# An RWKV-5 block followed by a mixture-of-depths layer on one core: chosen rows turned a unit later, turns one unit ahead, head and tail in another order

## The chip, the cores and the metric

The kernel runs on one core of one Trainium2 chip. The metric is device microseconds of one execution. TensorE is called PE here (its weight loads PEld), VectorE DVE, ScalarE ACT, GpSimd POOL and SyncE SP, as the profile calls them.

## The reference

```python
# r, k, v: (4, 8, 768, 48); w, u: (8, 48)
for t in range(S):
    cur = np.einsum('bhd,bhe->bhde', u[None] * kt, vt)
    y[:, :, t] = np.einsum('bhd,bhde->bhe', rt, state + cur)
    state = w[None, :, :, None] * state + np.einsum('bhd,bhe->bhde', kt, vt)
# x: y as (4, 768, 384); w_gate (384), w1 (384, 1024), w2 (1024, 384), capacity 128
scores = np.einsum('bsd,d->bs', x, w_gate)
out = x.copy()
for b in range(B):
    top_idx = np.argpartition(-scores[b], capacity)[:capacity]
    xe = x[b, top_idx]
    ye = np.maximum(xe @ w1, 0.0) @ w2
    g = 1.0 / (1.0 + np.exp(-scores[b, top_idx]))
    out[b, top_idx] = x[b, top_idx] + g[:, None] * ye
```

So a recurrence over 768 steps for 4 batches of 8 heads gives x; then, in each batch, the 128 rows with the highest scores go through a two-layer network and are written back.

## The kernel before

**Units.** The 4 x 768 rows are cut into 24 units of 128 rows, six to a batch; a unit holds all 8 heads in two chunks of 64 rows. In a unit the recurrence is written as matrix products: r is scaled by powers of w (`rh`), k by inverse powers (`kh` by the way of `kw`, which is k times `wk`), `scores` forms the chunks' r-by-k products in the PSUM tile `rp`, `masked` copies their lower triangle over a diagonal matrix `at` (which `diagonal` fills with the u-bonus `du` of the rows), `values_part` multiplies `at` with v into the PSUM tile `y`, `states_part` adds r times the state before the chunk, `state_sums` and `states` make the next state (`z`, `g`), and `decays` scales it by `wc` with four ACT instructions. `leave_y` copies `y` to `x` with three ACT copies and stores it; SP issues that store. `mark` is a one-element ACT copy of `y` that stands between `states_part` and `values_part`: the values products wait for it.

**Order.** The schedule is by hand (`manual_schedule`): each engine does its instructions in the order in which the code writes them, and waits only for data and buffers. The main loop runs over i = 0 to 24. Pass i (called unit i below) does `states_part`, `mark`, `values_part`, `leave_y` and the gate score for unit i-1, and scores, sums, states and mask for unit i; then it transposes on PE (`turn`, into `pk` and `pr`) and scales the k and r of a unit ahead (`turned_k` on ACT, `turned_r` on DVE); POOL does the bonus products `rk` and `rku` of unit i+2, `diagonal` and `scaled` (`kw`). Loads of r, k and v are issued by SP four units ahead.

**The second layer.** `score_row`, `compare_own` and `compare_others` compare the scores of a batch's blocks (`gt`); three passes after a batch's last unit, `rank` sums them on PE and DVE gives each row its rank (`qq`) and six one-hot blocks (`oh`); a pass later `pick` turns them to row numbers (`idx`) and `fetch` reads the 128 chosen rows (`xr`) from the output in HBM with an indirect DMA that POOL issues. `chosen` transposes `xr` on PE into `m`, ACT copies it to `xt`, and a queue of 16 pieces (8 `hidden`, 6 matmuls of the trace each, and 8 `expert`, 2 each) is taken out 3, 3, 2, 3, 3, 2 to a pass, behind the turns. `leave` adds the result to the rows and `store_rows` writes them back, also by POOL. Batch 3's second layer stands behind the loop (the tail).

**Places.** The dictionary `fill` and the list `counts` set the pass of each step of the second layer; `PARTS` the passes in which SP issues the eight weight loads; `pieces(m)` takes m pieces from the queue.

Of the kernel before, what the change touches and what calls it, by code (L numbers as in the profile page):

```python
# [17 lines left out]
def kernel(  # L18
# [29 lines left out]
    NIN, NV, NKW = 6, 8, 5  # L48
# [24 lines left out]
    wrow = const.tile([NP, 2, PAD], F32)  # L73
    ub = const.tile([128, H, D], F32)
# [13 lines left out]
    def load(n, which="krv"):  # L88
# [196 lines left out]
    SR, GT, RS, QQ, XR, XT, IDX, GA, HT, OH = {}, {}, {}, {}, {}, {}, {}, {}, {}, {}  # L285
    out_rows = out.rearrange("b s d -> (b s) d")

    def score_row(n):
        b, c = divmod(n, NC)
        if c == 0:  # L290
# [3 lines left out]
            nc.vector.tensor_copy(RS[b][:, 1, :], off)  # L294
# [16 lines left out]
    def rank(b):  # L311
        p = PM[:, 128 : 128 + NC]
        for c in range(NC):
            for cc in range(c, NC):
                nc.tensor.matmul(out=p[:, c : c + 1], lhsT=GT[b][:, cc, c, :], rhs=ones,
                                                   start=(cc == c), stop=(cc == NC - 1))
        rs = work.tile([128, NC], F32, name="rsum")
        nc.vector.tensor_add(rs, RS[b][:, 0, :], RS[b][:, 1, :])
        nc.vector.tensor_add(rs[:, 1:], rs[:, 1:], off[:, 1:])  # L319
        QQ[b] = work.tile([128, NC], F32, name="qq")  # L320
        nc.vector.tensor_add(QQ[b], p, rs)
# [89 lines left out]
    def store_rows():  # L411
        while LEFT:
# [52 lines left out]
    turn(PR, rpads[0])  # L465
    nc.vector.tensor_copy(tr[:, :, C + 1 : C + 2], PM[:, :NP][:, :, None])
# [138 lines left out]
```

## Time and profile before

| | us |
|---|---|
| median of 3 runs | 178.82 (177.78 to 180.06) |
| the profiled execution | 178.97 |
| its span, first to last instruction | 177.2 |
| PE busy | 142.8 (81%) |
| DVE busy | 115.3 (65%) |
| POOL busy | 108.6 (61%) |
| ACT busy | 71.7 (40%) |

The span is what the profile shows; 1.77 us of the execution lie around it. A busy share is a mean over stages with different limits, so the reading goes by stretches. In the page's groups and in the timeline, a line gives start or count, duration, engine, code line, what is written and what is read, and in brackets the idle time before it and what ended it; "issue" is time in which the engine waited for nothing that the profile shows.

### The profile page before, as it was taken

The page shows a single profiled execution, that of the slowest core. Times are in us where ns is not written, and L with a number is a line of the kernel's source. Part 1 is how long each engine was busy: PE and PEld are TensorE (multiplying, and loading weights), DVE is VectorE, ACT ScalarE, POOL GpSimd, SP SyncE. Part 2 cuts the span into 40 slices and gives each one's busy share as a digit, 9 for nine tenths or more (in the row PEclk, how much of TensorE's full clock was granted, in tenths as well). Part 3 has the DMA queues.
Part 4 walks back from the last instruction along what each step waited for, and adds up shares of the span by engine and source line. Part 5 has one row for each costly group of instructions (what it writes and reads, how often), then busy time and mean ns, then how long its engine had stood idle before and what let it go on. Part 6 is the DMA issues. An engine that isn't in the chain of part 4 may idle for free.

```text
span 177.2 us, 8283 instructions
## 1 busy us (share of the span) xinstructions
PE 142.8 (81%) x3605; PEld 121.4 (69%) x3605; DVE 115.3 (65%) x332; ACT 71.7 (40%) x243; POOL 108.6 (61%) x132
## 2 busy tenths in 40 slices
PE   1659977676977938999999599999997698939880
PEld 1448866566776828999777399997785596619740
DVE  6968568879699942679899634798997256520010
ACT  3114455452566542436466242465552443011100
POOL 5499999988599595289985970989936000040002
PEclk9999999998798796999999858999999999996998
DMA  6899998869899898777979770476113111020001
GB/s 109 175 206 190 182 216 179 176 138 244 178 249 238 178 265 209 166 171 207 238 168 195 196 169 13 113 156 141 48 48 93 50 48 45 0 93 0 0 0 44
DMA packets 81871, 24.51 MB, mean 138 GB/s; under 512 B 75564, under 2 KB 81452, under 8 KB 81836
## 3 DMA queue, kind: packets, MB, share of 16 engines
q1 hardware_dynamic: 81024, 22.03, 55.1%
q0 software_dynamic: 512, 1.57, 2.6%
q10 hardware_dynamic: 300, 0.39, 1.6%
q8 instruction: 28, 0.46, 1.1%
q14 instruction: 7, 0.06, 0.1%
HBM read 18.48 MB, written 5.51 MB: 135 GB/s over the span
## 4 chain that ended last, share of the span: by engine, by line
PE 37%; issue 25%; DVE 17%; DMA 11%; ACT 6%; POOL 1%; POOLq 1%; DVEq 0%
PE y L219 9%; DMA xr<-out_dram,idx 8%; PE e L393 7%; PE pk L191 5%; PE pr L191 4%; PE rp L205 4%; PE e L400 3%; PE rp L246 2%; ACT z L261 2%; DVE rh L195 2%; DVE gt L308 2%; DMA rpad<-in_r_dram 2%; DMA wrow<-in_w_dram 2%; DVE rsum L319 2%; DVE at L210 1%
## 5 line engine op out<-in xcount | busy, mean ns | idle before, releaser
L186 POOL TENSOR_TENSOR at<-dia,du 128x512 f32<-128x512 f32 x24 | 25.0, 1043 | 23.8 <-DVE du L182 13.2
L178 POOL TENSOR_TENSOR rku<-rk,ub 128x384 f32<-128x384 f32 x24 | 24.8, 1033 | 1.9
L176 POOL TENSOR_TENSOR rk<-rpad,kin 128x384 f32<-128x384 f32 x23 | 25.9, 1125 | 0.1
L195 DVE TENSOR_TENSOR rh<-pr,tr 128x512 f32<-128x512 f32 x24 | 16.4, 685 | 14.3 <-PE pr L191 14.0
L393 PE MATMUL e<-xt,w 128*128 128x128 f32 x162 | 23.5, 306 | 2.6 <-ACT xt L370 2.6
L393 PEld LDWEIGHTS e<-xt,w 128*128 128x128 f32 x162 | 22.4, 222 | 3.2 <-ACT xt L370 3.0
L219 PE MATMUL y<-vin,at 64*64 64x48 f32 x768 | 18.6, 227 | 6.5 <-issue 5.1
L400 PE MATMUL e<-w,ht 128*128 128x384 f32 x64 | 22.7, 490 | 0.4 <-ACT ht L396 0.4
L172 POOL TENSOR_TENSOR kw<-kin,wk 128x384 f32<-128x384 f32 x22 | 22.3, 1014 | 0.0
L205 PE MATMUL rp<-rh,kh 48*64 48x64 f32 x768 | 19.5, 232 | 3.2 <-issue 2.4
L270 ACT COPY x<-y 128x192 f32<-128x192 f32 x24 | 7.6, 318 | 35.5 <-PE y L219 34.3
L219 PEld LDWEIGHTS y<-vin,at 64*64 64x64 f32 x768 | 15.8, 142 | 7.8 <-issue 5.8
L261 ACT ACTIVATE z<-g,wc 128x48 f32<-128x48 f32 x80 | 20.2, 323 | 2.0 <-DVE g L255 1.6
L205 PEld LDWEIGHTS rp<-rh,kh 48*64 48x64 f32 x768 | 16.1, 145 | 4.6 <-issue 3.2
L191 PE MATMUL pk<-ident,kw 128*128 128x128 f32 x92 | 17.5, 321 | 1.8 <-DVE kw L172 1.8
L282 DVE SCALAR_TENSOR_TENSOR scr<-x,wg 128x384 f32<-128x384 f32 x24 | 17.2, 718 | 1.7 <-ACT x L272 1.6
L191 PE MATMUL pr<-ident,rpad 128*128 128x128 f32 x96 | 17.2, 309 | 0.9 <-DMA rpad<-in_r_dram 0.9
L210 DVE COPY_PREDICATED at<-mask,rp 128x512 f32<-128x512 uint32 x24 | 17.5, 730 | 0.0
L219 PE MATMUL y<-z,rh 48*64 48x48 f32 x704 | 16.9, 225 | 0.0
L301 DVE SCALAR_TENSOR_TENSOR gt<-m,sc,tri 128x128 bf16<-128x128 f32 x24 | 8.3, 347 | 13.2 <-ACT srow L297 12.2
L219 PEld LDWEIGHTS y<-z,rh 48*64 48x64 f32 x704 | 13.9, 137 | 4.4 <-issue 2.2
L358 POOL DMA_INDIRECT xr<-out_dram,idx x4 | 4.2, 1049 | 19.1 <-DVE idx L340 18.8
(88 smaller groups left out, 235.2 us busy)
## 6 DMA issues: line engine op xcount, KB each, us to landing
rpad<-in_r_dram SPq DMA_DIRECT2D x24, 192.0 KB, 3.6
vin<-in_v_dram SPq DMA_DIRECT2D x24, 192.0 KB, 4.8
out_dram<-x SPq DMA_DIRECT2D x24, 192.0 KB, 3.5
kin<-in_k_dram SPq DMA_DIRECT2D x23, 192.0 KB, 3.7
w<-in_moe_w_dram SPq DMA_DIRECT2D x8, 384.0 KB, 4.6
kpad<-in_k_dram SPq DMA_DIRECT2D x1, 192.0 KB, 2.8
ub<-in_u_dram ACTq DMA_DIRECT2D x1, 192.0 KB, 4.7
wg<-in_moe_w_gate_dram ACTq DMA_DIRECT2D x1, 192.0 KB
```

What stands on the lines that cost most here:

```text
L172: engine.tensor_mul(kws[n % NKW][:, :, :D], KIN[n], wk)
L176: nc.gpsimd.tensor_mul(rk, rpads[n % NIN][:, :, :D], KIN[n])
L178: nc.gpsimd.tensor_mul(RKU[n], rk, ub)
L186: nc.gpsimd.tensor_mul(AT[n], dia[:, None, :].to_broadcast([128, H, C]), DU[n].rearrange("t i p -> t (i p)")[:, :, None].to_broadcast([128 ...
L191: nc.tensor.transpose(dst[:, hp, :], src[:, 2 * hp : 2 * hp + 2, :], ident)
L195: nc.vector.tensor_mul(RH[n], PR, tr[:, :, :T])
L205: nc.tensor.matmul(out=RP[half(c), i, hp * C : (hp + 1) * C], lhsT=KH[n][head(i), hp, half(c)], rhs=RH[n][head(i), hp, half(c)], start=Tru ...
L210: nc.vector.copy_predicated(at, causal, RP[:, :, : NP * C].rearrange("s i (p t) -> s i p t", p=NP))
L219: nc.tensor.matmul(out=y_out(hp, i, c), lhsT=lhsT, rhs=rhs, start=(n, i, c) not in begun, stop=True, skip_group_check=True)
L261: nc.scalar.activation(Z0[n + 1][:, hp, :], G[n][:, hp, :], AF.Copy, scale=wc[:, hp : hp + 1])
L393: nc.tensor.matmul(out=pe[:, (f - f0) * 128 : (f - f0 + 1) * 128], lhsT=w1[:, d, f * 128 : (f + 1) * 128], rhs=XT[b, z][:, d, :], start=(d ...
L400: nc.tensor.matmul(out=PE[:, :Dm], lhsT=HT[b, z][:, f, :], rhs=w2[:, f, :], start=(f == 0), stop=(f == FB - 1))
```

## The change

It touches four things.

- **Second layer.** `chosen`, `enqueue` and `gates` of batches 0 to 2 move from pass e+5 to e+6 (e is the batch's last unit), and the six passes with pieces with them; `fetch` stays in pass e+4, but behind `diagonal` and ahead of `scaled` on POOL; `store_rows` writes only what an earlier pass left. "small" steps (ranks, pick, chosen) run ahead of the mask.
- **Turns.** k and r are turned one unit ahead instead of two, ahead of `decays`; `kw`, `kh`, `rh` and `vin` lose a buffer each. Sums stand before scores. In passes up to 9, four of a unit's eight diagonal blocks are made by ACT with a scaled copy each (`at` of 64 columns), the rest by POOL.
- **Head.** `u` and the gate vector come as one row each and are spread over the partitions by a product with a row of ones (`spread`); PE does 8, 3 and 3 transposes that nobody reads (`idle`); `kt` is made in halves and turned ahead of the first scores; no unit is turned in pass 0.
- **Tail.** The ranks of batch 3 are summed for blocks 0 to 4 first and for block 5 later; more hidden pieces, and six of the eight expert pieces, stand elsewhere. Weights come two passes later at first (7 to 14 instead of 5, 7 to 13).

```diff
-    NIN, NV, NKW = 6, 8, 5
+    NIN, NV, NKW = 6, 7, 4
...
-    nc.scalar.dma_start(
-        out=ub, in_=bass.AP(tensor=u.tensor, offset=u.offset, ap=[[0, 128], [D, H], [1, D]])
-    )
+    nc.scalar.dma_start(out=vecs[:, 0, :], in_=u.rearrange("h d -> (h d)")[None, :])
+    nc.scalar.dma_start(out=vecs[:, 1, :], in_=moe_w_gate[None, :])
...
+    def idle(m):
+        for _ in range(m):
+            nc.tensor.transpose(YP[:, 0, :128], ident, ident)
+
+
+    def spread(dst, j):
+        nc.tensor.matmul(out=PE[:, :Dm], lhsT=line, rhs=vecs[:, j, :], start=True, stop=True)
+        nc.scalar.copy(dst, PE[:, :Dm])
...
+    def diagonal(n, first=0):
         AT[n] = work.tile([128, H, C], F32, name="at", bufs=4)
...
+        for h in range(first):
+            nc.scalar.activation(AT[n][:, h, :], dia, AF.Copy, scale=du[:, h : h + 1])
+        if first < H:
+            nc.gpsimd.tensor_mul(AT[n][:, first:, :], dia[:, None, :].to_broadcast([128, H - first, C]),
+                                 du[:, first:, None].to_broadcast([128, H - first, C]))
...
-    def store_rows():
-        while LEFT:
+    def store_rows(m):
+        for _ in range(m):
...
-            at(e + 5, "small", chosen, b, z)
-            at(e + 5, "small", enqueue, b, z)
-            at(e + 5, "gate", gates, b, z)
+            at(e + 6, "small", chosen, b, z)
+            at(e + 6, "small", enqueue, b, z)
+            at(e + 6, "gate", gates, b, z)
         for j in range(6):
-            counts[e + 5 + j] = STEP[j % 3] * NST
...
-    PARTS = (5, 7, 8, 9, 10, 11, 12, 13)
+    PARTS = (7, 8, 9, 10, 11, 12, 13, 14)
...
+    idle(8)
     nc.tensor.transpose(PM[:, :NP], wrow.rearrange("p i d -> p (i d)"), ident[:NP, :NP])
     turn(PK, kpad)
+    nc.vector.tensor_copy(tr[:, :, C + 1 : C + 2], PM[:, :NP][:, :, None])
+    spread(ub.rearrange("t h d -> t (h d)"), 0)
+    idle(3)
     turn(PR, rpads[0])
+    idle(3)
...
     for i in range(NU + 1):
+        left = len(LEFT)
...
+        if 0 < i and i + 1 < NU:
+            turn(PK, kws[(i + 1) % NKW])
+            turned_k(i + 1)
+            turn(PR, rpads[(i + 1) % NIN])
+            turned_r(i + 1)
         if i < NU:
             decays(i)
-
-        run(i, "small")
-        if i + 2 < NU:
-            turn(PK, kws[(i + 2) % NKW])
-            turned_k(i + 2)
-            turn(PR, rpads[(i + 2) % NIN])
-            turned_r(i + 2)
...
-        if i + 1 < NU:
-            diagonal(i + 1)
-        if i + 3 < NU:
-            scaled(i + 3, nc.gpsimd)
+        if 0 < i and i + 1 < NU:
+            diagonal(i + 1, 4 if i < 10 else 0)
         run(i, "pool")
-        store_rows()
+        store_rows(left)
+        if 0 < i and i + 2 < NU:
+            scaled(i + 2, nc.gpsimd)
...
     b = B - 1
+    last = NC - 1
+    rank(b, PK[:, 0, :], range(last))
+    compare_others(NU - 1)
+    rank_base(b)
+    nc.vector.tensor_add(RB[b][:, :last], RB[b][:, :last], PK[:, 0, :last])
     pieces(2)
     score_row(NU - 1)
-    compare_others(NU - 1)
     compare_own(NU - 1)
-    pieces(2)
-    rank(b)
+    rank_more(b)
+    pieces(1)
+    rank(b, PM[:, 128 : 128 + NC], range(last, NC))
+    rank_sum(b, PM[:, 128 : 128 + NC])
+    pieces(1)
     for z in range(NST):
         one_hot(b, z)
-        pieces(2)
         pick(b, z)
         fetch(b, z)
     pieces(len(queue))
```

Three places show how the rows stand on an engine. First PE in pass 10, the one after batch 0's rows are fetched, before the change (`m` from `xr` is `chosen`, `e` from `xt` the first three hidden pieces):

```order
L205 MATMUL rp<-rh,kh 64x64 x16
L246 MATMUL rp<-vin,kw_87 48x48 x16
L219 MATMUL y<-vin,at 64x48 x16
L367 MATMUL m<-ident,xr 128x128 x3
L191 MATMUL pk<-ident,kw_89 128x128 x4
L191 MATMUL pr<-ident,rpad_81 128x128 x4
L393 MATMUL e<-xt,w_75 128x128 x9
L295 MATMUL m<-ident,sc_142 128x128
```

With the change pass 10 has no rows to turn; from its sums on it reads:

```order
L258 MATMUL rp<-vin,kw_91 48x48 x16
L217 MATMUL rp<-rh,kh 64x64 x16
L231 MATMUL y<-vin,at 64x48 x16
L203 MATMUL pk<-ident,kw_92 128x128 x4
L203 MATMUL pr<-ident,rpad_88 128x128 x4
L306 MATMUL m<-ident,sc_144 128x128
```

The transposes of `xr` and the hidden pieces follow in the same place of pass 11, so a whole pass now lies between the fetch and the first instruction that reads it; sums and scores have changed places.

Second ACT in pass 3, from the mark to the row of scores, before (`z` is `decays`):

```order
L232 COPY tiny<-y 1x1
L270 COPY x<-y 128x4x48
L271 COPY x<-y 64x4x48
L272 COPY x<-y 64x4x48
L261 ACTIVATE z_590<-g,wc 128x48 x4
L199 COPY kh<-pk 128x512
L297 COPY srow<-m 128x128
```

And with the change:

```order
L244 COPY tiny<-y 1x1
L282 COPY x<-y 128x4x48
L283 COPY x<-y 64x4x48
L284 COPY x<-y 64x4x48
L211 COPY kh<-pk 128x512
L273 ACTIVATE z_624<-g,wc 128x48 x4
L308 COPY srow<-m 128x128
L196 ACTIVATE at<-dia,du 128x64 x4
```

Four scaled copies now stand between the row of scores and the next pass's mark.

Third PE in the head, up to the first sums, before:

```order
L463 MATMUL m<-ident,wrow 128x4
L191 MATMUL pk<-ident,kpad 128x128 x4
L191 MATMUL pr<-ident,rpad_81 128x128 x4
L205 MATMUL rp<-rh,kh 64x64 x16
L484 MATMUL e<-ident,kt 128x128 x4
L191 MATMUL pr<-ident,rpad_82 128x128 x4
L191 MATMUL pk<-ident,kw_88 128x128 x4
L246 MATMUL rp<-vin,kw_87 48x48 x16
```

And with the change (`y` from `ident` are the products that nobody reads):

```order
L157 MATMUL y<-ident 128x128 x8
L489 MATMUL m<-ident,wrow 128x4
L203 MATMUL pk<-ident,kpad 128x128 x4
L161 MATMUL e<-vecs,line 128x384
L157 MATMUL y<-ident 128x128 x3
L203 MATMUL pr<-ident,rpad_83 128x128 x4
L157 MATMUL y<-ident 128x128 x3
L514 MATMUL m<-ident,kt 128x128 x4
L217 MATMUL rp<-rh,kh 64x64 x16
L203 MATMUL pr<-ident,rpad_84 128x128 x4
L203 MATMUL pk<-ident,kw_90 128x128 x4
L258 MATMUL rp<-vin,kw_89 48x48 x16
```

The transpose of `w` has eight unread ones ahead of it; the transposes of `kt` stand ahead of the first scores.

## Rows read from the trace of the kernel before

**Rows 1.** Busy time in stretches: PE, PEld, DVE, ACT, POOL, granted clock, DMA share, GB/s.

```profile
16.40:60.80 44.40, 35.65 (x1244) 31.45 (x1243) 36.37 (x97) 23.25 (x84) 38.09 (x43) 0.92 0.89 198
60.80:72.00 11.20, 7.55 (x161) 7.04 (x160) 5.04 (x16) 3.97 (x14) 7.69 (x9) 0.85 0.92 226
72.00:96.70 24.70, 24.55 (x747) 21.08 (x746) 21.29 (x62) 13.99 (x49) 18.83 (x19) 1.00 0.82 190
96.70:108.30 11.60, 9.03 (x159) 8.38 (x158) 5.16 (x16) 3.50 (x12) 8.02 (x10) 0.71 0.68 156
133.00:141.30 8.30, 5.54 (x151) 4.73 (x150) 4.54 (x15) 2.79 (x11) 2.64 (x5) 1.00 0.24 76
```

**Rows 2.** PE in order of time, where fetched rows are turned: start, duration, instruction.

```profile
67.08 0.87 PE L367 MATMUL m<-ident,xr 128*128 128x128 f32 x3 [3.19 <-DMA xr<-out_dram,idx]
...
74.83 2.17 PE L393 MATMUL e<-xt,w 128*128 128x128 f32 x18
...
102.27 0.88 PE L367 MATMUL m<-ident,xr 128*128 128x128 f32 x3 [1.37 <-DMA xr<-out_dram,idx]
...
104.65 3.62 PE L393 MATMUL e<-xt,w 128*128 128x128 f32 x18
...
139.01 2.27 PE L393 MATMUL e<-xt,w 128*128 128x128 f32 x18 [2.00 <-ACT xt L370]
```

**Rows 3.** The first fetch in the chain of waits: start, duration, what.

```profile
61.53 5.42 DMA xr<-out_dram,idx
```

**Rows 4.** PE's pauses in the scores, all of them: engine, line, total, times, longest.

```profile
PE rp L205 <- issue: 2.4, 6, 0.5
```

**Rows 5.** ACT in order of time, one early unit.

```profile
24.53 0.32 ACT L270 COPY x<-y 128x192 f32<-128x192 f32 x1 [1.84 <-PE y L219]
...
25.52 1.01 ACT L261 ACTIVATE z<-g,wc 128x48 f32<-128x48 f32 x4
...
27.19 0.15 ACT L232 COPY tiny<-y 1x1 f32<-1x1 f32 x1
```

**Rows 6.** PE in order of time, the values products of two early units.

```profile
24.12 0.37 PE L219 MATMUL y<-vin,at 64*64 64x48 f32 x10 [0.82 <-issue]
...
28.50 0.55 PE L219 MATMUL y<-vin,at 64*64 64x48 f32 x19 [0.67 <-issue]
```

**Rows 7.** The page's DMA queue that carries instructions: packets, MB, share.

```profile
q8 instruction: 28, 0.46, 1.1%
```

**Rows 8.** Groups of instructions by line: the scaled r, and the one-hot blocks.

```profile
L195 DVE TENSOR_TENSOR rh<-pr,tr 128x512 f32<-128x512 f32 x24 | 16.4, 685 | 14.3 <-PE pr L191 14.0
...
L331 DVE TENSOR_SCALAR oh<-slots,qq 128x128 bf16<-128x128 bf16 x24 | 5.2, 283 | 0.0
```

**Rows 9.** The head in the chain of waits: start, duration, what.

```profile
5.83 0.44 DVE tr L473
...
8.94 1.06 PE e L484 x4
...
10.02 0.49 ACT wk L486
...
10.53 2.01 DVE kw L172 x2
...
13.77 0.82 PE rp L246 x32
```

**Rows 10.** PE in order of time, in the head.

```profile
3.89 1.11 PE L191 MATMUL pk<-ident,kpad 128*128 128x128 f32 x4
...
19.93 0.66 PE L191 MATMUL pk<-ident,kw 128*128 128x128 f32 x4
```

**Rows 11.** PE in order of time, in the tail.

```profile
157.86 0.52 PE L367 MATMUL m<-ident,xr 128*128 128x128 f32 x3 [2.27 <-DMA xr<-out_dram,idx]
158.95 3.85 PE L393 MATMUL e<-xt,w 128*128 128x128 f32 x18 [0.57 <-ACT xt L370]
...
166.83 5.33 PE L400 MATMUL e<-w,ht 128*128 128x384 f32 x16
```

More of the change, by code (lines that the diff above doesn't have):

```diff
@@ L309, in compare_others, with rank, rank_base, rank_more @@
                                     op0=OP.is_ge, op1=OP.add, accum_out=RS[b][:, 1, c : c + 1])
[L311 to L314, printed above, removed]
+    def rank(b, p, blocks):
+        for c in range(blocks[-1] + 1):
+            own = [cc for cc in blocks if cc >= c]
+            for cc in own:
                 nc.tensor.matmul(out=p[:, c : c + 1], lhsT=GT[b][:, cc, c, :], rhs=ones,
[L316 to L319, printed above, removed]
-        QQ[b] = work.tile([128, NC], F32, name="qq")
-        nc.vector.tensor_add(QQ[b], p, rs)
+                                 start=(cc == own[0]), stop=(cc == own[-1]))
+    def rank_base(b):
+        RB[b] = work.tile([128, NC], F32, name="rbase")
+        nc.vector.tensor_add(RB[b][:, 1:], RS[b][:, 1, 1:], off[:, 1:])
+        nc.vector.tensor_copy(RB[b][:, 0:1], off[:, 0:1])
+    def rank_more(b):
+        nc.vector.tensor_add(RB[b], RB[b], RS[b][:, 0, :])
+    def rank_sum(b, p):
+        QQ[b] = work.tile([128, NC], F32, name="qq")
+        nc.vector.tensor_add(QQ[b], p, RB[b])
+    def ranks(b):
+        rank(b, PM[:, 128 : 128 + NC], range(NC))
+        rank_base(b)
+        rank_more(b)
+        rank_sum(b, PM[:, 128 : 128 + NC])
     def one_hot(b, z):
@@ L447 @@
         e = b * NC + NC - 1
-        at(e + 3, "small", rank, b)
+        at(e + 3, "small", ranks, b)
         for z in range(NST):
@@ L473, with back @@
     nc.vector.tensor_mul(tr[:, :, :C], tr[:, :, C:T], winv[:, :, None].to_broadcast([128, NP, C]))
-    back = bass.AP(tensor=tr.tensor, offset=tr.offset + T - 1, ap=[tr.ap[0], [T + 1, NP], [-1, T]])
-    KH[0] = work.tile([128, NP, T], F32, name="kh", bufs=3)
-    nc.vector.tensor_mul(KH[0], PK, back)
+    def back(lo, n):
+        return bass.AP(tensor=tr.tensor, offset=tr.offset + T - 1 - lo, ap=[tr.ap[0], [T + 1, NP], [-1, n]])
+    for c in range(2):
+        nc.scalar.copy(kt[:, :, half(c)], back(c * C, C))
+    KH[0] = work.tile([128, NP, T], F32, name="kh")
+    nc.vector.tensor_mul(KH[0], PK, back(0, T))
     turned_r(0)
-    nc.scalar.copy(kt, back)
-    nc.vector.tensor_mul(wc, tr[:, :, T], tr[:, :, T])
     bonus(0)
-    bonus_sum(0)
-    scores(0)
-    for hp in range(NP):
-        nc.tensor.transpose(PE[:, hp * 128 : (hp + 1) * 128], kt[:, hp, :], ident)
-    turn(PR, rpads[1])
-    nc.scalar.copy(wk, PE.rearrange("s (p i d) -> s (p i) d", i=2, d=PAD)[:, :, :D])
-    diagonal(0)
-    scaled(0, nc.vector)
-    scaled(1, nc.vector)
+    for hp in range(NP):
+        nc.tensor.transpose(PM[:, hp * 128 : (hp + 1) * 128], kt[:, hp, :], ident)
+    nc.scalar.copy(wk, PM.rearrange("s (p i d) -> s (p i) d", i=2, d=PAD)[:, :, :D])
+    scores(0)
+    turn(PR, rpads[1])
+    scaled(1, nc.vector)
+    bonus_sum(0)
+    scaled(0, nc.gpsimd)
     turn(PK, kws[1])
     turned_k(1)
+    diagonal(0, 4)
+    turned_r(1)
+    nc.vector.tensor_mul(wc, tr[:, :, T], tr[:, :, T])
     bonus(1)
-    turned_r(1)
     load(2)
     load(3)
-    scaled(2, nc.gpsimd)
-    bonus_sum(1)
-    nc.vector.tensor_scalar(tri, jp, 0.0, None, op0=OP.is_lt)
-    gate_vector()
+    iotas()
     for i in range(NU + 1):
+        left = len(LEFT)
         if i + 4 < NU:
             load(i + 4)
-        if i == 1:
-            iotas()
         if i in PARTS:
@@ L564 @@
     pieces(len(queue))
-    store_rows()
+    store_rows(len(LEFT))
     for z in range(NST):
@@ L570 @@
         pieces(len(queue))
-        store_rows()
+        store_rows(len(LEFT))
 _INS = ['r', 'k', 'v', 'w', 'u', 'moe_w_gate', 'moe_w1', 'moe_w2', 'moe_capacity']
```

47 lines of the change are left out of this document (30 added, 17 removed).

## The prediction

> **What bounds the kernel now.** I read the busy time by stretches first, then PE's timeline where a stretch is not full, then what PE waits for there.
>
> [Rows 1] cut the loop into stretches of units. Units 11 to 15 (72.00 to 96.70) are full: PE is busy 24.55 of 24.70 us, 4.94 a unit, and units 17 to 21 give the same 24.70. There PE is the bound and nothing is to be had except by taking work from it. The stretches in between are not full. Unit 10 took 11.20 us, unit 16 11.60 and unit 22 8.30, for work that in the full stretches takes about 5.5 (4.94, and the turning of fetched rows, 0.52 [rows 11]). [Rows 2] say why: PE stands before `chosen`, 3.19 and 1.37 us on the fetched rows and in the third case 2.00 on the copy behind them. The transfer of rows took 5.42 us [rows 3], longer than the rest of a unit that was to cover it. And the loss goes on behind the wait: the same 18 hidden matmuls take 3.62 us after the second stall and 2.17 in a full unit [rows 2], at a granted clock of 0.71 and 0.85 in those stretches [rows 1], so partly at 1.2 GHz. The rest is PE's pauses in the scores, which stand beside POOL's indirect DMAs: 2.4 us over the run [rows 4].
>
> Units 1 to 9 (16.40 to 60.80) take 4.93 each with PE busy 35.65 of 44.40. No engine is full, but one cycle closes in each unit: ACT copies y to x, then z, kh, the score row and the mark, 24.53 to 27.34, 2.81 us [rows 5]; then the 32 values products, of which 19 take 0.55 [rows 6], some 0.65, with hand-overs 0.75; then x again. That is 3.56; the unit has more because PE pauses for 0.82 and 0.67 us in the middle of the values products [rows 6]. POOL, at 38.09 of 44.40 [rows 1], is close behind.
>
> The pauses of [rows 6] end 4.38 us and 128 matmuls apart (10 + 9 for turns and score row + 96 + 13), which with their weight loads is 256 instructions; the instruction queue moved 0.46 MB in 28 packets, 16 KB each [rows 7]. So I take them for the fetch of the next block of PE's instructions, late while the loads keep the DMA engines 0.89 busy [rows 1]. The Trainium skill (Runtime: NRT & Kernel Launch, Instruction fetch mechanics) has the blocks of 256 instructions too, but says that crossing one is mostly hidden. The rows speak against the second half; by the page the term for units 1 to 9 below would be the cycle alone, -2.2 instead of -0.8, and the time 160.6.
>
> **The change, part by part.** The sum is made against the profiled execution: span 177.2, 1.77 around it, 178.97; the median of the runs shown, 178.82, is 0.15 less.
>
> *Second layer a unit later.* The fetch is issued in pass 9 as before, and PE reads the rows in pass 11: a whole unit of at least 4.5 us lies between, with what is left of pass 9. 5.42 us of transfer are covered unless they grow by half. The pieces are not fewer: each batch's six passes hold 3, 3, 2, 3, 3, 2. So units 11 to 16 are the full stretch of 24.70 and one unit more of three hidden pieces and the turned rows, 5.5: 30.2; units 17 to 22 the same; 60.4. The pauses beside the indirect DMAs stay, since the fetches and stores stay, and now fall into full units: +2.4. Unit 10 has no pieces and all its diagonals on POOL, like an early unit: 4.6 (the 4.38 of [rows 6] by 137/128 matmuls is 4.69; ACT's cycle 3.56 is below). Units 10 to 22: 67.4, against 11.20 + 24.70 + 11.60 + 24.70 + 8.30 = 80.5: **-13.1**. `store_rows` a pass later and the fetch ahead of `kw` put 1 us of POOL's issue ahead of a `kw` that PE turns a unit later: nothing, while POOL has slack (18.83 of 24.70 [rows 1]). Ranks ahead of the mask hold back scores of the next unit by under 1 us; in full units the pieces cover it.
>
> *Turns one unit ahead.* Scores of a unit now need kh and rh of the same pass before. From the end of the values products: two turns, 1.1 (one takes 0.66 [rows 10], and they overlap), and rh 0.69 [rows 8] behind them, 1.8 us; ahead of the scores PE has to wait for the three copies of x (0.99, 24.53 to 25.52 [rows 5]) and does states and sums (some 0.9), 1.9. It fits with 0.1 to spare in the early units and by 2 us of pieces in the full ones. Nothing, and between +0 and +0.5 a unit if DVE is late.
>
> *Units 1 to 9.* POOL loses half of each diagonal, and ACT gets four scaled copies. The nearest row is four scalings of 48 columns in 1.01 us [rows 5]; I take 0.98 in the chain. They lie in the cycle, ahead of the mark: 3.56 + 0.98 = 4.54. Against that, PE's stream shifts: 14 unread transposes and the product for u come, eight turns of pass 0 go, some 8 matmuls in all, and each unit moves the block's edge by 9. So the edge leaves the values products by about unit 4 and falls into scores, where ACT's longer cycle hides it. Bounds: no pause, 9 x 4.54 = 40.9 and 1.3 for the first ranks' one-hot blocks (5.2 in four batches [rows 8]), 42.2; a pause of 0.82 in each, 49.6. I take 4.70 a unit, near the block's 4.69, and 1.3: 43.6 against 44.4: **-0.8**, from -2.2 to +5.2.
>
> *Head.* Eight unread transposes stand ahead of that of w: four took 1.11 [rows 10], so eight are 2.2, and they can start when the identity is there, which I put 1.0 ahead of PE's first transpose now, so the powers of w end 1.2 later, at 7.5 instead of 6.27 [rows 9]. From there the change is shorter. Now 2.67 us lie between that and kt's transposes at 8.94 [rows 9], scores among them; with the change only ACT's two copies of kt, for which I allow 0.8 (two of the 0.32 that a copy of a like size takes [rows 5], and hand-overs). Four transposes 1.06 and wk 0.49 bring wk to 9.9 instead of 10.51. From there to unit 1 at 16.40 are 5.9 now: the second `kw` goes to POOL (-0.7 of 2.01), and the two turns of unit 2 that fill the time from the end of the sums, 14.59, to 16.40 go (-1.8), of which I keep 0.4 for the first state. Unit 1 at 13.7: **-2.7**. If the unread products bring PE to 2.4 GHz before (0.66 instead of 1.11 for four transposes [rows 10]) it is -3.4; if POOL, which must do two `kw`, six bonus products and three half diagonals before unit 2's turn, comes later, -1.9. u's single row frees DMA time that nothing waits for.
>
> *Tail.* Unit 23 gets the turning of rows and PE's wait for their copy, 0.52 + 0.57 [rows 11]: +1.1. Three more hidden pieces, 2.17 [rows 2], stand behind unit 24. But six expert pieces instead of two now lie over the last fetch, 4.0 us at 5.33 / 8 = 0.67 each [rows 11], so PE's wait of 2.27 goes; 0.5 of it comes back where one expert piece alone lies beside the one-hot blocks: +0.4. The 18 hidden matmuls behind it then take 2.17 instead of 3.85 [rows 2, 11]: -1.7. Together **-0.2**.
>
> Weights two passes later move DMA work from units 5 to 13 to 7 to 14; pass 11 is the first that reads them, and reads the first half. No term.
>
> Sum: -2.7 - 0.8 - 13.1 - 0.2 = -16.8: span 160.4, execution 162.2, and 0.15 less for the median: **162.0 us**, 9.4% faster.
>
> **Rivals.** (a) *ACT becomes the early bound.* The four copies sit in the cycle and the block's edge stays in the values products: +5.2 - (-0.8) = 6.0 at most, half of it likely: 165 to 168. For it: both pauses shown lie there now; against it: the shift of the edge. (b) *The stall moves.* The fetched rows or the weights come late under denser loads, or PE still drops to 1.2 GHz at pass 11: half of the 13.1 is lost, 168.5. Against it: 4.5 us more cover. (c) *Better.* The scores' pauses go, the head runs at 2.4 GHz, early units at 4.54: 162.0 - 2.4 - 0.7 - 1.4 = 157.5. (d) *Slower than before.* rh and kh one unit ahead come late in every unit, because DVE reaches rh only behind mask and ranks; each of 23 units then pays. It decides from 16.8 / 23 = 0.73 us a unit; at 0.9 it gives 182.7. Against it: DVE is busy 21.29 of 24.70 in the full units, PE has 2 us of pieces there, and the early units' slack is used up only by a DVE that is late by a third of its unit.
>
> **How the numbers follow.** Forecast 0.64 (its own terms reach 158 to 165), (a) 0.15, (b) 0.09, (c) 0.08, (d) 0.04. The range 156 to 169 holds all but (d) and the far ends of (a) and (b). About 2% is what a measurement of this kernel can tell from no change; only (d) and the worst of (b) lie there: faster 0.93, same 0.04, slower 0.03.
>
> **What would show it.** Right: no wait of PE on the fetched rows in passes 11, 17 and 23, stretches of 24.7 us and 30 for six units, granted clock near 1.00 from 60 us on; unit 1 at 13 to 14 us; early units at 4.7 with ACT's at-copies ahead of the mark; the last 18 hidden matmuls of the first group in 2.2 us. Wrong: early units over 5 us with ACT nearly full, PE waiting in scores for rh, or a granted clock under 0.9 in the middle.

## The result and the profile after

Four executions of the changed kernel gave 166.54 to 171.34 us, median 168.99; four of the kernel before, three of them those shown ahead, a median of 179.44. The ratio is 0.937 (0.917 to 0.957): faster, as forecast, but 7 us above the 162.0 predicted and only 0.01 inside the upper end of the range. The ratio leaves out executions more than 1.5% above the shortest of their kernel, the profiled one of the changed kernel (171.34, span 169.6) among them. A second profiled execution of the same code, the first experiment below, took 165.92 (span 164.2); the two are read side by side. In that group of runs the two shortest executions are 165.92 and 166.69, of the kernel before 174.11 and 176.19: a ratio of 0.95.

The kernel before was profiled in an execution of 178.97, and its later ones go from 174.1 to 184.7. So a term that is measured against that one profile holds to about 1.5 us: units 1 to 9 took 44.40 in it and 42.92 in before_late below, with the same code up to there.

Busy time in stretches of the first one (columns as in [rows 1]), cut at the starts of units 1, 10, 11, 12, 17, 18, 19 and 23:

```profile
0.00:12.69 12.69, 11.10 (x101) 8.66 (x102) 7.50 (x25) 3.34 (x7) 6.96 (x22) 1.00 0.92 180
12.69:56.91 44.22, 35.38 (x1263) 30.08 (x1252) 38.32 (x100) 33.93 (x126) 37.71 (x47) 0.96 0.85 185
56.91:61.14 4.23, 3.83 (x138) 3.25 (x137) 4.23 (x9) 3.36 (x15) 4.03 (x4) 1.00 0.90 203
61.14:71.84 10.70, 8.78 (x143) 8.27 (x142) 6.84 (x19) 3.59 (x12) 8.44 (x9) 0.68 0.92 215
71.84:98.08 26.24, 25.12 (x759) 21.25 (x758) 23.40 (x62) 15.14 (x53) 20.20 (x21) 1.00 0.93 214
98.08:103.45 5.37, 5.37 (x144) 5.14 (x143) 5.16 (x12) 2.34 (x8) 4.68 (x6) 1.00 0.78 181
103.45:112.38 8.93, 6.86 (x156) 6.49 (x155) 6.72 (x15) 3.43 (x12) 6.42 (x7) 0.81 0.71 157
112.38:132.27 19.89, 19.40 (x604) 16.14 (x603) 18.48 (x51) 11.63 (x41) 12.72 (x15) 1.00 0.21 62
132.27:169.60 37.33, 28.94 (x341) 22.09 (x340) 11.20 (x43) 6.88 (x22) 4.36 (x7) 0.99 0.10 34
```

The same of the second one, cut at units 1, 10, 11, 12, 17 and 23:

```profile
12.80:56.84 44.04, 34.61 (x1262) 29.55 (x1252) 37.06 (x100) 33.81 (x126) 37.86 (x47) 0.96 0.86 190
56.84:61.08 4.24, 3.99 (x139) 3.31 (x138) 4.24 (x9) 3.37 (x15) 4.04 (x4) 1.00 0.98 261
61.08:68.06 6.98, 6.09 (x144) 5.53 (x143) 6.91 (x18) 3.59 (x13) 6.58 (x7) 1.00 0.96 224
68.06:95.31 27.25, 25.49 (x759) 21.45 (x758) 23.51 (x64) 15.26 (x53) 23.36 (x25) 1.00 0.94 223
95.31:126.79 31.48, 30.09 (x901) 26.26 (x900) 29.56 (x77) 17.38 (x60) 22.76 (x25) 1.00 0.44 108
126.79:164.20 37.41, 28.97 (x341) 22.10 (x340) 11.20 (x43) 6.89 (x22) 4.38 (x7) 0.98 0.10 34
```

The forecast's terms in both:

| stretch | forecast, change | first | second |
|---|---|---|---|
| head, to unit 1 | -2.7 | 12.69 - 16.40 = -3.7 | -3.6 |
| units 1 to 9 | -0.8 | 44.22 - 44.40 = -0.2 | -0.4 |
| units 10 to 22 | -13.1 | 75.36 - 80.5 = -5.1 | -10.5 |
| from unit 23 | -0.2 | 37.33 - 35.9 = +1.4 | +1.5 |
| span | -16.8 | -7.6 | -13.0 |

So the early part came out within half a us of what was added up, the tail is 1.6 to 1.7 dearer, and the term of units 10 to 22 is short by 2.6 to 8. In that stretch the waits of [rows 2] are gone: PE turns the fetched rows without a wait on their DMA. What stands there now is seen in PE's timeline of unit 11, first execution:

```profile
61.14 0.31 PE L231 MATMUL y<-z,rh 48*64 48x48 f32 x2
61.88 0.32 PE L231 MATMUL y<-z,rh 48*64 48x48 f32 x6 [0.43 <-DVE z L264]
63.70 0.88 PE L231 MATMUL y<-z,rh 48*64 48x48 f32 x22 [1.49 <-issue]
...
66.85 0.91 PE L392 MATMUL m<-ident,xr 128*128 128x128 f32 x3
...
69.25 2.55 PE L418 MATMUL e<-xt,w 128*128 128x128 f32 x18
```

and in the second:

```profile
61.82 0.67 PE L231 MATMUL y<-z,rh 48*64 48x48 f32 x30 [0.43 <-DVE z L264]
...
64.59 0.55 PE L392 MATMUL m<-ident,xr 128*128 128x128 f32 x3
...
65.85 2.17 PE L418 MATMUL e<-xt,w 128*128 128x128 f32 x18
```

Both wait 0.43 us for the state `z`, which DVE makes late. Only the first has the pause of 1.49 us after eight products of the unit ("issue": no semaphore ends it), and behind it the turns and hidden products run partly at 1.2 GHz, at a granted clock of 0.68 in that unit. Pause and lower clock cost 3.7 us between two executions of one code.

The DMA packets of the traces say what ends this pause. The queue that carries instructions [rows 7] moves 28 packets of 16 KB, one for every 127 matmul records or so, and PE's long pauses stand at just these distances. In unit 11 of five profiles (the last three are kernels below):

| profile | packet lands | PE goes on | between | pause |
|---|---|---|---|---|
| changed, first | 62.44 | 63.70 | 1.25 | 1.49 |
| changed, second | 60.54 | not held up | | 0 |
| one_input | 61.77 | 63.21 | 1.44 | 2.62 |
| gates_later | 63.00 | 64.32 | 1.31 | 3.15 |
| fetch_last | 63.07 | 64.54 | 1.48 | 3.34 |

It is so in all 14 profiles: 104 pauses of 0.15 us or more stand at these places, and each ends 1.23 to 1.66 us after such a packet has landed; the few at other places are at most 0.46. PE's 3623 matmuls and as many weight loads are some 28 times 256 instructions. So the long pauses are waits for PE's next block of instructions, as the forecast took them. What makes a packet late is another question (fewer_loads, below).

Unit 18 of the first execution, on DVE, POOL, ACT and PE:

```profile
102.04 3.10 DVE L294 SCALAR_TENSOR_TENSOR scr<-x,wg 128x384 f32<-128x384 f32 x1
...
105.19 1.22 DVE L399 SCALAR_TENSOR_TENSOR scr<-xr,wg 128x384 f32<-128x384 f32 x1
```

```profile
101.69 1.04 POOL L440 DMA_INDIRECT out_dram<-ot,idx  x1 [0.16 <-issue]
102.75 1.01 POOL L179 TENSOR_TENSOR kw<-kin,wk 128x384 f32<-128x384 f32 x1
103.71 1.01 POOL L183 TENSOR_TENSOR rk<-rpad,kin 128x384 f32<-128x384 f32 x1
104.79 1.20 POOL L185 TENSOR_TENSOR rku<-rk,ub 128x384 f32<-128x384 f32 x1
```

```profile
106.45 0.20 ACT L401 ACTIVATE gate<-gsum 128x1 f32<-128x1 f32 x1 [2.51 <-DVE scr L399]
106.56 0.25 ACT L308 COPY srow<-m 128x128 f32<-128x128 f32 x1
106.83 0.15 ACT L244 COPY tiny<-y 1x1 f32<-1x1 f32 x1
```

```profile
107.04 0.69 PE L231 MATMUL y<-vin,at 64*64 64x48 f32 x32 [2.07 <-ACT tiny L244]
...
109.42 2.93 PE L418 MATMUL e<-xt,w 128*128 128x128 f32 x18
```

Read backwards: PE waits 2.07 us for the mark, which waits on ACT behind the sigmoid of the gates, which waits for DVE's gate score of the chosen rows, which stands behind the unit's own gate score, 3.10 us long where 0.55 is the shortest. It ends 0.4 us after POOL's short gap between rk and rku (104.72 to 104.79). In the second profile the unit's own gate score got in ahead of POOL (0.55), that of the chosen rows took 2.67 in its place, and PE waited 0.97 for the mark. In the groups by line the 24 gate scores took 17.2 us (718 ns each) in the kernel before, and here:

```profile
L294 DVE SCALAR_TENSOR_TENSOR scr<-x,wg 128x384 f32<-128x384 f32 x24 | 27.5, 1145 | 1.3 <-ACT x L284 1.3
```

### The profile page after: what moved, and what is told of

Its sections match the earlier page's. It is cut to its first block, busy times and chain, and to the rows that moved or that the text cites. A ratio compares the mean times of both kernels' runs of the same rounds, so it can differ in the third digit from the quotient of the medians.

```text
span 169.6 us, 8431 instructions
## 1 busy us (share of the span) xinstructions
PE 144.8 (85%) x3623; PEld 121.4 (72%) x3623; DVE 121.8 (72%) x332; ACT 83.7 (49%) x290; POOL 105.5 (62%) x133
## 4 chain that ended last, share of the span: by engine, by line
DVE 31%; PE 29%; issue 21%; ACT 8%; POOL 6%; DMA 2%; POOLq 1%; DVEq 0%; ACTq 0%
DVE scr L294 8%; PE y L231 6%; PE pk L203 4%; PE e L418 4%; PE e L425 4%; PE pr L203 4%; DVE at L222 3%; DVE rh L207 3%; DVE gt L319 3%; DVE oh L356 2%; DVE du L189 2%; PE rp L217 2%; DVE gt L312 2%; DVE z L264 2%; ACT at L196 2%
## 5 line engine op out<-in xcount | busy, mean ns | idle before, releaser
L198 POOL TENSOR_TENSOR at<-dia,du 128x512 f32<-128x512 f32 (+1 forms) x24 | 20.3, 846 | 21.6 <-DVE du L189 21.5
L294 DVE SCALAR_TENSOR_TENSOR scr<-x,wg 128x384 f32<-128x384 f32 x24 | 27.5, 1145 | 1.3 <-ACT x L284 1.3
L185 POOL TENSOR_TENSOR rku<-rk,ub 128x384 f32<-128x384 f32 x24 | 26.1, 1088 | 3.4 <-ACT ub L162 1.6
L231 PE MATMUL y<-vin,at 64*64 64x48 f32 x768 | 16.9, 226 | 6.9 <-ACT tiny L244 6.9
L418 PE MATMUL e<-xt,w 128*128 128x128 f32 x162 | 21.2, 287 | 1.4 <-ACT xt L395 1.1
L418 PEld LDWEIGHTS e<-xt,w 128*128 128x128 f32 x162 | 20.3, 203 | 1.9 <-ACT xt L395 1.6
L231 PEld LDWEIGHTS y<-z,rh 48*64 48x64 f32 x704 | 14.6, 138 | 9.0 <-issue 5.4
L231 PE MATMUL y<-z,rh 48*64 48x48 f32 x704 | 18.1, 227 | 3.2 <-issue 2.2
L231 PEld LDWEIGHTS y<-vin,at 64*64 64x64 f32 x768 | 14.5, 141 | 8.3 <-ACT tiny L244 8.2
L203 PE MATMUL pr<-ident,rpad 128*128 128x128 f32 x96 | 16.8, 304 | 0.0
L425 PEld LDWEIGHTS e<-w,ht 128*128 128x128 f32 x64 | 11.4, 190 | 7.1 <-issue 0.8
L211 ACT COPY kh<-pk 128x512 f32<-128x512 f32 x23 | 13.5, 587 | 4.4 <-PE pk L203 3.8
```

The source lines that it names most:

```text
L185: nc.gpsimd.tensor_mul(RKU[n], rk, ub)
L198: nc.gpsimd.tensor_mul(AT[n][:, first:, :], dia[:, None, :].to_broadcast([128, H - first, C]), du[:, first:, None].to_broadcast([128, H - ...
L203: nc.tensor.transpose(dst[:, hp, :], src[:, 2 * hp : 2 * hp + 2, :], ident)
L231: nc.tensor.matmul(out=y_out(hp, i, c), lhsT=lhsT, rhs=rhs, start=(n, i, c) not in begun, stop=True, skip_group_check=True)
L294: nc.vector.scalar_tensor_tensor(scr, X[n], 1.0, wg, op0=OP.mult, op1=OP.mult, accum_out=sc[b][:, c : c + 1])
L418: nc.tensor.matmul(out=pe[:, (f - f0) * 128 : (f - f0 + 1) * 128], lhsT=w1[:, d, f * 128 : (f + 1) * 128], rhs=XT[b, z][:, d, :], start=(d ...
```

## The experiments

Twelve kernels, in three groups, each beside the kernel before on the same chip (medians of before 179.5, 178.5 and 177.7). Executions of one kernel lie up to 6.5 us apart, those of the kernel before up to 10.6, so the readings come from stretches of the profiles; medians are given beside them, and no median alone tells one changed kernel from another.

**The changed kernel once more.**

> The changed kernel itself once more, for a second profile. Theory A, the gate score waits for POOL (a multiply of two SBUF tiles on VectorE stands still while POOL runs its own multiplies back to back): the same three gate scores behind an indirect DMA take 2.8 to 3.1 us again instead of 0.55, their lines sum to some 27 us, and units 11 and 18 are long again (10.7 and 8.9 us). Theory B, the losses of units 11 and 18 belonged to that one execution: these units take 5.5 to 6 here and the span is 162 to 163. Time expected by A 167 to 169, by B 163 to 164.

168.4 us. Both theories had part of it: four gate scores of 2.0 to 2.9 us again, one of them that of chosen rows (the 24 of the units take 994 ns in the mean), so these belong to the code; unit 18 took 6.24, not 8.9, and unit 11 6.98, not 10.7, so the larger part of those two losses belonged to that execution.

**The second layer's place: alone, and undone.**

```diff
 # before_late: kernel before;  early5: changed kernel, the other way
-            at(e + 5, "small", chosen, b, z)      # and enqueue, gates, counts
+            at(e + 6, "small", chosen, b, z)
```

> The kernel before with only the second layer a unit later (chosen, the queue of pieces and the gates at e + 6 instead of e + 5). By the forecast's term for units 10 to 22 it gains 13.1 us there, and loses about 1 in the tail, where the turning of the last fetched rows moves in: ratio 0.93, 167 us. If the gate scores that wait for POOL, or PE's pauses for its instructions, take back half of that term, as in the changed kernel: ratio 0.955 to 0.96, 171 to 172. If the stall only moves to the next unit: 0.99 to 1.

> The changed kernel with only the second layer moved back (chosen, the queue of pieces and the gates at e + 5 as before; head, turns, diagonals, fetch order, weights and tail as changed). If the gain of the change is the second layer's place, which alone brought the kernel before from 179.5 to 169.5: the waits on the fetched rows are back, units 10, 16 and 22 take over 8 us, the time is 177 to 180. If the other parts carry a gain of their own, as the forecast's -2.7 and -0.8 say: 175 to 176.

169.5 and 169.35 us; the first lies between its two forecasts, the second below both of its own. The later place alone takes the kernel before to within about 1 us of the changed kernel by medians and to within some 2 by the shortest executions (168.1 to 170.1 against 165.9 and 166.7; against the kernel before its ratio is 0.968, 0.939 to 0.997). Undone in the changed kernel it costs as much, not 6 to 10. The gains don't add.

The later place by itself, in the kernel before, cut at units 10, 11, 17 and 23:

```profile
58.97:63.20 4.23, 3.61 (x139) 3.14 (x138) 3.33 (x12) 1.88 (x8) 3.94 (x6) 1.00 0.85 234
63.20:96.99 33.79, 30.82 (x902) 26.49 (x901) 26.64 (x78) 18.64 (x65) 28.18 (x29) 1.00 0.91 212
96.99:127.92 30.93, 29.94 (x893) 25.66 (x892) 26.04 (x76) 16.51 (x58) 23.33 (x24) 1.00 0.46 111
127.92:166.30 38.38, 28.50 (x341) 21.58 (x340) 10.98 (x41) 7.09 (x24) 4.64 (x7) 1.00 0.11 37
```

Units 10 to 22 take 68.95 instead of 80.5: -11.5 of the 13.1, with 1.0 us of waiting on fetched rows left in the whole run (6.8 before) and 1.33 us of a pause in unit 11. From unit 23 on it pays 2.5. So the forecast's largest term is nearly right where it stands alone; in the changed kernel the other edits take part of it back.

The stretches of the undone kernel (cut at units 10, 11, 16, 17, 22, 23) and PE at its first turned rows:

```profile
57.77:69.89 12.12, 8.93 (x160) 8.35 (x160) 7.65 (x17) 5.02 (x21) 8.26 (x8) 0.72 0.84 210
...
94.73:104.88 10.15, 7.09 (x160) 6.82 (x159) 7.31 (x16) 3.25 (x12) 8.68 (x10) 0.83 0.63 148
...
129.40:135.47 6.07, 5.75 (x160) 5.36 (x159) 5.69 (x16) 3.25 (x12) 3.43 (x6) 1.00 0.25 78
135.47:169.10 33.63, 25.77 (x320) 19.30 (x319) 9.71 (x38) 6.18 (x20) 3.32 (x5) 0.99 0.10 35
```

```profile
63.68 0.88 PE L392 MATMUL m<-ident,xr 128*128 128x128 f32 x3 [2.96 <-DMA xr<-out_dram,idx]
```

The stall is back in units 10 and 16 (in 16 the wait of 3.06 ends with DVE's mask, not with the rows), hardly in 22. Units 10 to 22 take 77.7, so the later place is worth 2.3 to 7.8 there (75.36 and 69.95); but from unit 23 on the undone kernel needs 33.6 where the changed one needs 37.4. 3.8 us are given back in the tail, where DVE, ACT and POOL are busy for less than a third of the time.

**Gate scores behind POOL.** Four kernels.

```diff
 # one_input
-        nc.vector.scalar_tensor_tensor(scr, X[n], 1.0, wg, op0=OP.mult, op1=OP.mult,
+        nc.vector.tensor_scalar(scr, X[n], 1.0, 0.0, op0=OP.mult, op1=OP.add,
 # wg_psum_early
+        nc.vector.scalar_tensor_tensor(scr, X[n], 1.0, PE[:, :Dm] if n < 10 else wg, op0=OP.mult, op1=OP.mult,
 # gates_later: wg_psum_early, and
-            at(e + 6, "gate", gates, b, z)
+            at(min(e + 8, NU), "gate", gates, b, z)
 # fetch_last
+        if 0 < i and i + 2 < NU:
+            scaled(i + 2, nc.gpsimd)
         run(i, "pool")
         store_rows(left)
-        if 0 < i and i + 2 < NU:
-            scaled(i + 2, nc.gpsimd)
```

> The changed kernel with gate scores that are plain sums of a row: the multiplication by the gate vector is left out, so the instruction reads one SBUF tile and not two; everything else, the ranks and the fetches of as many rows among it, stays. Theory A (gate scores wait for POOL because of their second SBUF operand, and that is on the path): each takes 0.55 us, units 1 to 9 fall from 44.2 to about 42, units 11 and 18 lose 2 to 3 us each, the time is 161 to 164. Theory C (ACT's four at-copies are what holds the early units, and half clock after PE's pauses for instructions is what holds units 11 and 18; the long gate scores lie beside idle time): gate scores of 0.55, but the time within 1 us of the changed kernel's, 168.

> The changed kernel, in which the gate scores of units 0 to 9 read the gate vector from PSUM bank e, where its spreading product has left it (nothing else uses that bank before unit 11's pieces): one SBUF operand for these ten units, two from unit 10 on. Theory A: gate scores of units 0 to 8 fall from 0.84 to 1.38 us to about 0.6, units 1 to 9 from 44.2 to 42, units 11 and 18 stay long; time 1.5 to 2.5 below the changed kernel. Theory C: gate scores as short, units 1 to 9 within 0.5 of 44.2.

> The changed kernel with two edits at once: the gate scores of units 0 to 9 read the gate vector from PSUM, and the gates of the chosen rows stand two passes later (e + 8), out of the pass in which the stored rows' DMA, the unit's gate score and the gates meet on POOL and DVE and ACT's sigmoid keeps the mark of the next unit waiting. If that chain is what makes unit 18 long (6.2 and 8.9 us in two executions of the changed kernel): unit 18 at 5.0 to 5.5, and the time 1 to 3 below the changed kernel's 168.4. If not: unit 18 at 6 or over, time within 1 us.

> The changed kernel with the fetch of chosen rows and the store of finished ones behind the scaled keys (kw) on POOL, as in the kernel before, and not ahead of them. Theory A': in the changed order POOL goes from the indirect DMA straight into two multiplies, and VectorE's gate score, which has two SBUF operands, stands until the short gap between rk and rku, 2.7 to 3.1 us; z, the mask and the gates on ACT then come late in passes 11 and 18. With the fetch last no gate score takes over 1.4 us, unit 18 is 5.0 to 5.5, units 11 and 12 lose the wait on z, time 1 to 2.5 below the changed kernel's 168.4. If the gate scores are short but the units as long: the time stays within 1 us, and the long gate scores lie beside other waits.

169.85, 168.95, 171.97 and 169.18 us: by the medians none is better than the changed kernel, and the gains of 1 to 7 us that were expected are not there (fetch_last has the shortest two executions of all, 164.7 and 164.9, and three over 170; whether its order is the better one stays open). The gate scores did what was expected: 541 ns each with one operand, 545 for the ten that read PSUM, and none over 1.42 us with the fetch last. So the long ones come from the second SBUF operand and POOL. The Trainium skill (SBUF — State Buffer, Who interferes with whom) says that a VectorE instruction with two SBUF inputs contends with a GpSimd instruction that reads SBUF, and calls such contention an exclusive lock; these runs agree, with 541 ns for one input against 994 and 1145 for two.

Where the time went instead is seen in units 11 and 12. PE's timeline with the fetch last:

```profile
60.87 0.33 PE L231 MATMUL y<-z,rh 48*64 48x48 f32 x8
64.54 0.88 PE L231 MATMUL y<-z,rh 48*64 48x48 f32 x22 [3.34 <-issue]
...
75.80 0.34 PE L231 MATMUL y<-vin,at 64*64 64x48 f32 x9 [1.64 <-issue]
...
77.07 3.72 PE L418 MATMUL e<-xt,w 128*128 128x128 f32 x18
```

with gate scores of one operand:

```profile
63.21 0.51 PE L231 MATMUL y<-z,rh 48*64 48x48 f32 x21 [2.62 <-issue]
...
74.79 0.39 PE L231 MATMUL y<-vin,at 64*64 64x48 f32 x9 [2.57 <-issue]
```

The pause stands at the same eighth product of unit 11 as in the changed kernel, and again 253 matmul records further on, in unit 12. So the profiles are compared in two parts, units 11 and 12, and all the rest of the span (starts of units from PE's timeline):

| kernel | span | PE's pauses in units 11, 12 | units 11, 12 | the rest | unit 18 |
|---|---|---|---|---|---|
| changed, first | 169.6 | 1.5 | 15.8 | 153.9 | 8.9 |
| changed, second | 164.2 | 0 | 12.3 | 151.9 | 6.2 |
| fewer_loads | 164.0 | 0 | 11.9 | 152.1 | 6.6 |
| at_pool | 164.8 | 0.4 | 11.7 | 153.1 | 6.5 |
| last_early | 167.1 | 1.0 | 14.0 | 153.1 | 6.1 |
| gates_later | 168.3 | 3.5 | 16.0 | 152.3 | 6.0 |
| no_idle | 168.2 | 3.5 | 17.9 | 150.3 | 7.4 |
| wg_psum_early | 167.6 | 3.5 | 17.6 | 150.0 | 6.6 |
| both | 164.5 | 2.2 | 14.6 | 149.9 | 5.2 |
| one_input | 168.7 | 5.3 | 19.5 | 149.2 | 5.1 |
| fetch_last | 168.7 | 5.0 | 20.0 | 148.7 | 5.1 |

Units 11 and 12 take some 12 us without a pause and mostly 1.1 to 2.5 us more for each us of pause; what is above 1 goes with a lower clock behind it.

Unit 18 takes 5.1 to 5.2 in one_input, fetch_last and both, where no gate score is over 1.3 us in passes 15 to 17, and 6.0 or more in the others of the table. There PE's own record settles the cause: it waits 0.82 to 2.07 us for the mark in all seven profiles that have the changed order on POOL, the gates in pass 17 and a gate score of two SBUF operands behind the store, and not at all in one_input, fetch_last, both and gates_later, nor in before_late, which has the old order on POOL. In gates_later unit 18 has a pause of 0.66 for instructions in its 6.0 instead.

What the gate scores cost over the whole run is not shown. Outside units 11 and 12 one_input, fetch_last and both take 148.7 to 149.9, but wg_psum_early 150.0 and no_idle 150.3 (with 0.9 of its head), and the changed kernel itself differs by 2 between its two executions. PSUM operands in units 0 to 9 do not shorten units 1 to 9: 43.4 in wg_psum_early, 44.35 in gates_later with the same edit and 44.1 in one_input, against 44.0 and 44.2; there most of the waiting lies beside ACT's cycle, as the second theory said.

**Fewer loads.**

```diff
+            if n > 8:
+                VIN[n] = VIN[8]
+                return
```

> The changed kernel without the loads of v for units 9 to 23 (these units multiply unit 8's v instead, which is left out of the computation), so a third of the loads is gone from pass 5 on; instructions of PE, ACT, DVE and POOL as before. Theory D: PE's pauses in passes 11 to 13, up to 2.6 us each with half clock behind them, are the fetch of its instructions held up by DMA engines that are 0.9 busy. Then the pauses over 0.3 us between 56 and 80 us go, units 11 and 12 take 11 to 12 us together in place of 12.3 to 19.5, and the time is 161 to 164. Theory E: these losses have nothing to do with the loads (VectorE behind POOL, ACT's order): units 11 and 12 stay at 12 to 19, the time at 167 to 169.

167.22 us. The profiled execution is as theory D said: no pause in units 11 and 12, 11.9 us for both, at a DMA share of 0.80 where the second profile of the changed kernel has 0.96. But that one has no pause there either, and the other executions without the loads (166.1 to 169.5) are no shorter. What speaks for theory D is the whole run: pauses for instructions add up to 0.8 us here and to 3.2 to 10.7 in the other 13 profiles. In unit 11 the packet starts 1.3 us after PE passed the place before, where it starts 2.1 to 4.3 us after in the kernels of the table, but for at_pool, where it starts after 0.9 with all loads. That loads make the packets late is thus likely, and not shown.

**All diagonals on POOL.**

```diff
-            diagonal(i + 1, 4 if i < 10 else 0)
+            diagonal(i + 1)
```

> The changed kernel with all diagonals on POOL, none of the at-copies on ACT. The forecast's rival (a), ACT's four copies hold the early units: the cycle falls from 4.54 to 3.56 and units 3 to 10 from 4.5 to about 4.2, where POOL (1.00 + 1.00 + 1.00 + 1.04 us a unit and hand-overs) becomes the next bound; time 1.5 to 2.5 lower. The other view, POOL is as near the bound as ACT: units 3 to 10 stay at 4.5 or grow, gate scores wait longer behind POOL, the time is the same or up to 2 us longer.

167.88 us. Units 4 to 7 take 4.32 each where the changed kernel takes 4.58 in most; so ACT's copies do set the early period, by 0.25. But POOL is then busy 16.24 of 16.55 us in units 3 to 6, DVE's comparison and with it `pick` wait behind it, unit 9 takes 6.8 in place of 4.6, and unit 11 starts at 63.54, not 61.1. Units 1 to 9 together take 46.4, not 44.0: the gain of each unit is lost again in the same stretch.

**The third batch early, and both edits.** last_early sets `m = e + (6 if b < B - 2 else 5)` for the second layer's steps; both has that and fetch_last's order.

> The changed kernel, where only the last batch inside the loop (the third) has its second layer a unit earlier again (chosen in pass 22 and not 23), the first two as changed. The third batch's rows are fetched when the DMA engines are 0.2 to 0.3 busy, and moving it late put three more pieces and the turning of rows behind the loop: unit 23 took 6.3 instead of 4.2, and from unit 24 to the end 31.1 instead of 29.4. So unit 22 should grow by 2.5 to 3 (pieces, turning, a wait for the rows under 1), unit 23 and the tail shrink by 3.7: time 1 lower, 0.5 to 2.5. If the wait on the rows is back in full (2 to 3 us with half clock): 1 to 3 higher.

> The edits of fetch_last and last_early together: if each gives what its theory expects, 2 to 4 us below the changed kernel, 164.5 to 166.5; if VectorE behind POOL is not on the path and the tail's gain is given back in unit 22, 168.

168.9 and 169.05 us. Unit 22 grew to 8.25 and 8.6 and what follows fell from 37.4 to 33.6: together 41.8 and 42.2, against 41.7 in the changed kernel. The expected 1 us is not there: the pieces of the second and third batch meet in unit 22. This move did not save the tail's price.

**No unread transposes.** All three `idle` calls are taken out.

> The changed kernel without the fourteen unread transposes. The forecast's step: eight of them stand ahead of w's transpose and delay the powers of w by 1.2 us, so without them unit 1 would start 1 us earlier, at 11.7. The trace of the changed kernel says otherwise: they run from 1.52 to 3.49, and w's transpose starts at 3.58, when its row has come in; then without them unit 1 starts no earlier, and later by what PE loses at half clock in the head, 0.5 to 1 us: 13.3 to 13.8, time the same within 1 us.

170.53 us. PE in the head with them (changed kernel, second profile), then without:

```profile
7.95 0.85 PE L157 MATMUL y<-ident 128*128 128x128 f32 x3
8.59 1.06 PE L514 MATMUL m<-ident,kt 128*128 128x128 f32 x4
...
12.80 0.28 PE L231 MATMUL y<-nothing,rh 48*64 48x48 f32 x2
```

```profile
7.61 1.11 PE L511 MATMUL m<-ident,kt 128*128 128x128 f32 x4
...
11.86 0.28 PE L231 MATMUL y<-nothing,rh 48*64 48x48 f32 x2
```

The start of 11.86 is near the forecast's 11.7, but not by its way. The first eight delay nothing (w's transpose starts at 3.57 and 3.58); the other six stand ahead of `kt`, which goes at 7.61 without them and at 8.42 to 8.59 in the profiles with them. For unit 1 the gain is less sure: it starts at 11.98 to 12.80 with them, as PE comes to 2.4 GHz (0.60 instead of 1.06 to 1.11 for four transposes) at different points of the head. The median is no lower, and the profile has 17.9 us in units 11 and 12. One of its pauses shows something else: that of unit 12, 2.70 us, stands at the same count of PE's matmul records as in one_input and fetch_last (1744), and so, with fourteen transposes gone ahead of it, fourteen matmuls later in the program, in the turn of r instead of the values products. So its place goes by the count of instructions and not by what PE does there.

## Why the prediction was right, and where it was short

- **The number.** The median lies 0.01 inside the range and outside the 158 to 165 that the forecast's own terms were to reach; 9.4% was forecast, 6.3 and 5% were measured. That the range held is luck, by the width that the rivals gave it. What follows goes by terms.
- **The second layer a unit later, -13.1.** The mechanism was right: the wait on the fetched rows is gone, and the later place alone gives -11.5. In the changed kernel the size was wrong: -10.5 and -5.1. Two steps were mis-sized. One is "The pauses beside the indirect DMAs stay, since the fetches and stores stay, and now fall into full units: +2.4": in units 10 to 22 nothing and 0.24 us of these are left. The other is that units 11 to 16 were taken as a full stretch, so that PE's waits for instructions were priced for units 1 to 9 alone. The kernel before has none behind 52.02; in its stalls the next packets landed up to 6.3 us ahead of PE. Without the stall they cost units 11 and 12 from nothing to 8 us (11.7 to 20.0 for both) where about 10.5 was allowed. A cost that the forecast did not have at all, the gate score behind POOL, is worth some 1 us in unit 18 of the second profile.
- **"Nothing, while POOL has slack"** for the fetch ahead of `kw` was another error: POOL has slack, but the new order leaves no gap behind the indirect DMA, and it is DVE that pays (2.7 to 3.1 us against at most 1.4 with the old order).
- **Tail, -0.2: +1.5 measured.** The wait on the last fetch went and the hidden pieces run in 2.27 us, as said. Unit 23 takes 6.3 instead of 5.3, with a pause of 0.41; what is behind it saved 0.6 instead of 1.3.
- **Head, -2.7: -3.6 and -3.7.** A little beyond its bound of -3.4. The 1.2 us of delay by eight transposes were not there: they start 2.2 us ahead of PE's first transpose of before (1.52 against 3.73), not 1.0, and end at 3.49, ahead of the row of w. Without that delay the sum gives -3.9. The other six, which had no price, hold `kt` back by 0.8 to 1.0.
- **Units 1 to 9, -0.8: -0.2 and -0.4.** Right in mechanism: ACT's copies set a period of 4.58, and the pauses moved from the values products into the scores (4.5 us there in the second profile), where they cost little. The number says little: the same code differs by 1.5 between before and before_late.
- **Rivals.** (a) is excluded as a loss: ACT's cycle holds the early units, yet all diagonals on POOL gain nothing. (d) is excluded: rh is not waited for unit by unit. (b), given 9 in 100, came nearest with its 168.5: PE does fall to 1.2 GHz at pass 11 in the first profile, though behind late instructions and not behind late rows or weights.

So [rows 6, 7] were read rightly ahead: PE's long pauses are waits for its instructions. Why a packet comes 0.9 us after PE passed the place before it or 4.3 stays open in part; that loads hold it up is argued from fewer_loads and not shown. The Trainium skill (Runtime: NRT & Kernel Launch, Instruction fetch mechanics), weighed ahead, calls crossing a block mostly hidden. By count the traces agree, with a pause at 7 and 9 of the 27 places in the two profiles of the changed kernel; by size they do not, with up to 3.34 us at one place.

## What to carry to other kernels

When a stall is removed, price the stretch by what the next wait can be, not by a full stretch elsewhere: the later second layer alone took 10 us off the median, the other edits without it 9 and both together 11 (6, 7 and 8 by the shortest executions), and work moved a unit later came back as 3.8 us in the tail. Look at what follows an instruction on POOL as closely as at POOL's load: a vector multiply with two SBUF operands took up to 3.1 us there where POOL left no gap. Where a pause has no releaser, look for what its end follows: here a packet of the instruction queue. With executions that differ by 5 us, compare kernels by stretches, and keep the one that varies apart.

## What the runs showed of the hardware

- DVE's gate score of 0.55 us took 2.7 to 3.1 where POOL went from an indirect DMA into two multiplies: in the case shown it ended 0.4 us after the gap of 0.07 us behind rk, and not at the change from kw to rk (103.7), where the two overlap by 0.05. With the gate vector in PSUM, or left out, it took 0.54.
- PE paused 0 to 3.34 us at one and the same product of unit 11, in executions and kernels that issue the same number of instructions up to there.
- In 14 profiles all 104 such pauses, 127 matmul records apart or a multiple of it, end 1.23 to 1.66 us after a packet of 16 KB of the instruction queue has landed; the packets themselves take 0.9 to 2.5 us.
